# Chunk pairs taken from one batch, fewer and larger loads, and a reordered scan in a fused state-space scan and feed-forward kernel

## The chip, the cores and the metric

The kernel runs on one core of one Trainium2 chip. The metric is the time of one execution in device microseconds. The kernel before takes 173.81 us, the median of three runs between 173.72 and 175.98. The engines are named as in the profile: PE is the matrix engine and PEld its weight loads, DVE the vector engine, ACT the scalar engine, POOL the general-purpose engine, and SP the engine that here only issues transfers. A q behind the name (SPq, ACTq) marks an instruction that issues a DMA.

## The reference

Two layers follow each other. The first is a chunked state-space scan over 4 batches, 8 heads, 768 tokens, with 32 channels of x and 16 of state per head:

```python
for c in range(nc):                       # the reference's chunks have 32 tokens
    cum = np.cumsum(la, axis=-1)          # la = log(clip(a))
    L = np.exp(cum[:, :, :, None] - cum[:, :, None, :]) * causal
    CB = np.einsum('bhin,bhjn->bhij', Cc, Bc)
    y_intra = np.einsum('bhij,bhjd->bhid', CB * L, xc)
    y_inter = np.einsum('bhin,bhnd->bhid', Cc, state) * np.exp(cum)[:, :, :, None]
    y[:, :, sl] = y_intra + y_inter
    Bx = np.einsum('bhjn,bhjd->bhjnd', Bc, xc) * decay_from_j[:, :, :, None, None]
    state = decay_full[:, :, None, None] * state + np.sum(Bx, axis=2)
```

The second takes the 3072 rows of 256 that the scan leaves and is a feed-forward layer with 2048 hidden units:

```python
h = np.maximum(x @ w_in, 0.0)
return (h * h @ w_out).astype(np.float32)
```

## The kernel before, in words

**Units.** A unit of work, a pair, is 256 tokens: one 128-token chunk `c` of two neighbouring batches (`PAIRS`, L106). There are 12 pairs. On the 128 partitions lie 64 token couples of one batch and 64 of the other. The products of decays are made once for all chunks (L318 to L327): `P_sb` is the running product of `a` inside a chunk, `Pinv` its reciprocal, `Ptot` the product of a whole chunk.

**The scan of a pair k** has these phases. `ph_load` (L111) issues the loads of B, C and x on SP, two DMAs per tensor, one for each batch. `ph_prep` (L139) multiplies C by `P_sb` into `cz`, casts B into `Bb`, and multiplies x by `Pinv` into `xs`; from pair 1 on, all three on POOL. `ph_tr` (L162) transposes with six matmuls into PSUM, and DVE copies the result out as `bct` (L171). `ph_mt` (L178) makes the 16 products of C and B, and `ph_mask` (L194) multiplies them by the causal mask on DVE, in four parts, into `mts`. `ph_y` (L202) has 16 matmuls with the old state (L213), 16 that make the state's increment (L224), and 32 that apply `mts` to `xs` (L234). `ph_T` (L244) casts the result on ACT into `T`, and `ph_state` (L251) updates the state on DVE with an addition (L263) and a multiplication (L264).

**One buffer.** `tr`, `mt` and `Y` are all tiles of the tag "A" in the pool `ps_s`, which has one buffer of four PSUM banks. Each of them therefore waits until the one before it has been read to the end.

**The feed-forward of a pair** is eight steps. A step (blk, fp) is `mm1` (L270): four matmuls of 256 columns into `hps` (two buffers), a relu on ACT into `hb` (L278), and a square on DVE into `h2` (L280). `mm2` (L283) is four matmuls (L290) that add a step's part to `ops`. After the eighth step ACT copies `ops` to `osb` (L295) and SP issues four DMAs to the output (L298).

**Order.** It is written out by hand, and every engine works through its own list in that order. The start (L308 to L361 or so) runs pairs 0 and 1 through the scan one behind the other; between their phases ACT issues the loads of the weights, eight DMAs for `w_in` and one for `w_out` in each of five portions (`load_w`, L126), and casts the portions to bf16 (`cast_w`, L302; `w_out` on POOL). Then a loop runs over 96 steps:

```python
mm1(*steps[s])
for fn, args in todo.pop(s, []):
    fn(*args)
if s >= LAG:
    mm2(*steps[s - LAG])
```

`mm2` runs LAG = 3 steps behind `mm1`. The first 16 steps alternate between pairs 0 and 1. The scan of pair k is hung into steps from s0 = 8k - LEAD on, with LEAD = 10: `ph_tr` at s0, `ph_mt` at s0 + 1, the masks at s0 + 2 to s0 + 5, `ph_y` at s0 + 6, `ph_T` and `ph_state` at s0 + 7; `ph_prep` is at s0 - 4 and `ph_load` at s0 - 12.

**Waits of transfers.** The transfers of SP and ACT share eight completion semaphores in turn, so a DMA is issued only when the eighth DMA before it has landed.

## Time and profile before

| What | Value |
|---|---|
| median of the runs | 173.81 us |
| profiled execution, its own time | 173.16 us |
| its span, first to last instruction | 171.4 us |
| PE busy | 111.3 us, 65% |
| PEld busy | 89.5 us, 52% |
| DVE busy | 85.8 us, 50% |
| ACT busy | 72.6 us, 42% |
| POOL busy | 32.0 us, 19% |
| moved by DMA | 14.19 MB in 46,403 packets |
| mean granted clock of PE | 0.995 |

No engine is busy for more than two thirds of the span. The span has a start in which the feed-forward does not run yet, a long middle in which one pair's scan and another's feed-forward go side by side, and a short end. What limits each is read from the waits and the timeline of that stretch, not from the shares of the whole. Busy time of PE counts overlapping matmuls as long as any of them runs, and their ends are modelled.

### The profile page before, as it was taken

How to read it: one execution, taken by the hardware profiler on the slowest of the kernel's cores; microseconds unless marked ns; L12 is line 12 of the kernel's file. 1: busy time of each engine (PE TensorE's matmuls, PEld its weight loads, DVE VectorE, ACT ScalarE, POOL GpSimd, SP SyncE). 2: the span in 40 equal slices, each digit the busy share in tenths (PEclk: the TensorE clock that was granted, in tenths of full speed). 3: DMA queues.
4: the chain of work that ended last, by engine and by line, in shares of the span. 5: the costliest groups of instructions: out<-in, count | busy, mean ns of one | idle time of the engine just before them, and what ended most of it. 6: DMA issues, size and time to landing. Idle time of an engine off the chain costs nothing.

```text
span 171.4 us, 4268 instructions
## 1 busy us (share of the span) xinstructions
PE 111.3 (65%) x1740; PEld 89.5 (52%) x1740; DVE 85.8 (50%) x182; ACT 72.6 (42%) x129; POOL 32.0 (19%) x46
## 2 busy tenths in 40 slices
PE   0132012304976896968958869689685897979970
PEld 0021010203865685756746758568574786768850
DVE  2218007002767474595565745848459455492420
ACT  2001010014855474453535734546346354566740
POOL 4026101502940000314230502204022000000000
PEclk9999999999999999999999999999999999999998
DMA  4775979596000004645624235252351102011012
GB/s 94 144 169 108 198 158 237 106 259 190 2 4 0 4 3 95 136 84 127 115 64 79 53 76 111 46 95 49 78 109 33 33 0 64 3 31 34 18 43 61
DMA packets 46403, 14.19 MB, mean 83 GB/s; under 512 B 39568, under 2 KB 45616, under 8 KB 46384
## 3 DMA queue, kind: packets, MB, share of 16 engines
q1 hardware_dynamic: 42080, 9.54, 29.0%
q10 hardware_dynamic: 4304, 4.39, 8.9%
q8 instruction: 13, 0.21, 0.5%
q14 instruction: 6, 0.05, 0.1%
HBM read 10.77 MB, written 3.15 MB: 81 GB/s over the span
## 4 chain that ended last, share of the span: by engine, by line
PE 32%; DVE 28%; DMA 17%; ACT 10%; issue 5%; SPq 2%; ACTq 2%; DVEq 0%
DVE mts L196 13%; PE ops L290 12%; DVE h L280 11%; PE hps L275 10%; DMA x_nat<-in_x_dram 6%; ACT hb L278 5%; ACT T L247 3%; DMA w_out_f<-in_moe_w_out_dram 3%; DMA w_in_f<-in_moe_w_in_dram 3%; DMA C_nat<-in_C_dram 3%; PE Y L213 2%; PE mt L185 2%; SPq L119 2%; PE Y L234 2%; DMA B_nat<-in_B_dram 2%
## 5 line engine op out<-in xcount | busy, mean ns | idle before, releaser
L278 ACT ACTIVATE hb<-hps 128x512 bf16<-128x512 f32 x96 | 57.5, 602 | 56.6 <-PE hps L275 56.4
L280 DVE TENSOR_TENSOR h<-hb 128x512 bf16<-128x512 bf16 x96 | 45.7, 477 | 47.5 <-ACT hb L278 47.5
L275 PE MATMUL hps<-T,w_in_b 128*128 128x256 bf16 x384 | 59.0, 278 | 9.2 <-ACT T L247 9.2
L290 PE MATMUL ops<-w_out_b,h 128*128 128x256 bf16 x384 | 57.4, 273 | 0.0
L275 PEld LDWEIGHTS <-w_in_b 128*128 128x128 bf16 x384 | 38.1, 99 | 14.9 <-issue 9.7
L290 PEld LDWEIGHTS <-h 128*128 128x128 bf16 x384 | 35.5, 98 | 6.8 <-issue 2.0
L196 DVE TENSOR_TENSOR mts<-mt,cb 128x512 bf16<-128x512 f32 x48 | 32.2, 682 | 2.2 <-PE mt L185 2.2
L144 POOL TENSOR_TENSOR cz<-C_nat,P_sb 128x256 bf16<-128x256 f32 x11 | 7.9, 717 | 57.9 <-DMA C_nat<-in_C_dram 50.7
L166 PE MATMUL tr<-cb,Bb 128*128 128x128 bf16 x24 | 5.0, 230 | 18.8 <-DVE S L260 8.2
L156 POOL TENSOR_TENSOR xs<-x_nat,Pinv 128x512 bf16<-128x512 f32 x12 | 13.7, 1141 | 14.0 <-DMA x_nat<-in_x_dram 12.8
L213 PE MATMUL Y<-bct,S 32*32 32x128 bf16 x160 | 4.0, 216 | 13.7 <-DVE mts L196 13.7
L169 PEld LDWEIGHTS <-cz 128*128 128x128 bf16 x48 | 4.0, 104 | 15.0 <-issue 15.0
L213 PEld LDWEIGHTS <-S 32*32 32x32 bf16 x160 | 3.1, 90 | 15.6 <-issue 15.6
L303 ACT CAST w_in_b<-w_in_f 128x1024 bf16<-128x1024 f32 (+1 forms) x5 | 4.3, 869 | 15.0 <-DMA w_in_f<-in_moe_w_in_dram 15.0
L260 DVE TENSOR_TENSOR S<-Y,Ptot 128x128 bf16<-128x128 f32 x2 | 0.6, 292 | 18.7 <-ACT T L247 18.7
L171 DVE COPY bct<-tr 128x768 bf16<-128x768 bf16 x12 | 6.7, 556 | 5.2 <-PE tr L169 5.2
L247 ACT CAST T<-Y 128x512 bf16<-128x512 f32 x12 | 7.0, 582 | 5.4 <-DMA w_in_f<-in_moe_w_in_dram 5.4
L304 POOL CAST w_out_b<-w_out_f 128x1024 bf16<-128x1024 f32 (+1 forms) x5 | 4.3, 867 | 25.7 <-DMA w_out_f<-in_moe_w_out_dram 16.5
L295 ACT COPY osb<-ops 128x512 f32<-128x512 f32 x12 | 7.0, 583 | 1.2 <-PE ops L290 1.2
L185 PE MATMUL mt<-bct 32*64 32x256 bf16 x192 | 5.7, 303 | 2.2 <-DVE bct L171 2.1
L234 PE MATMUL Y<-mts,xs 64*32 64x128 bf16 x384 | 6.3, 233 | 0.0
L224 PE MATMUL Y<-xs,Bb 64*32 64x64 bf16 x160 | 2.6, 202 | 5.4 <-DVE mts L196 5.4
(28 smaller groups left out, 36.3 us busy)
## 6 DMA issues: line engine op xcount, KB each, us to landing
x_nat<-in_x_dram SPq DMA_DIRECT2D x24, 128.0 KB, 3.2
out_dram<-osb SPq DMA_DIRECT2D x48, 64.0 KB, 2.1
B_nat<-in_B_dram SPq DMA_DIRECT2D x24, 64.0 KB, 2.7
C_nat<-in_C_dram SPq DMA_DIRECT2D x24, 64.0 KB, 2.9
w_in_f<-in_moe_w_in_dram ACTq DMA_DIRECT2D x24, 64.0 KB, 3.2
w_out_f<-in_moe_w_out_dram ACTq DMA_DIRECT2D x3, 512.0 KB, 4.7
w_in_f<-in_moe_w_in_dram ACTq DMA_DIRECT2D x16, 32.0 KB, 2.7
w_out_f<-in_moe_w_out_dram ACTq DMA_DIRECT2D x2, 256.0 KB, 4.2
```

What stands on the lines that cost most here:

```text
L144: e_c.tensor_tensor(out=_fap(czk, 0, [[144, 4], [32, 4], [1, 16]]), in0=_fap(t["C"][:, 0, :], 0, [[16, 4], [64, 4], [1, 16]]), in1=_fap(P_ ...
L156: e_x.tensor_tensor(out=_fap(xs[:, 0, :], 0, [[256, 2], [32, 8], [1, 32]]), in0=_fap(t["x"][:, 0, :], 0, [[32, 2], [64, 8], [1, 32]]), in1 ...
L185: nc.tensor.matmul(mt[64 * u:64 * u + 64, q, r, :, :], bct[32 * q:32 * q + 32, r, 0, u * 64:u * 64 + 64], _fap(bct[32 * q:32 * q + 32, 0, ...
L196: nc.vector.tensor_tensor(out=v["mts"][:, q], in0=v["mt"][:, q], in1=_fap(cb[:, 128:129], 0, [[128, 2], [0, 2], [1, 128]]), op=ALU.mult)
L213: nc.tensor.matmul(Y[32 * q:32 * q + 32, u, g * 128:(g + 1) * 128], S_b[32 * q:32 * q + 32, u, g * 32:(g + 1) * 32], ct_ap(v["bct"], q, g, u),
L234: nc.tensor.matmul(Y[32 * q:32 * q + 32, u, g * 128:(g + 1) * 128], v["xs"][64 * u:64 * u + 64, r, (2 * q + g) * 32:(2 * q + g) * 32 + 32] ...
L247: nc.scalar.copy(out=_fap(t[:, 0, :], 0, [[128, 2], [256, 2], [1, 128]]), in_=Y[:, 0:2, 0:256].rearrange("p u (g i) -> p u g i", g=2))
L275: nc.tensor.matmul(hps[:, j, :], w_in_b[:, g, f * 128:(f + 1) * 128], T[blk][:, g, :], start=(g == 0), stop=(g == 1), skip_group_check=True)
L278: nc.scalar.activation(out=hb, in_=hps, func=AF.Relu)
L280: nc.vector.tensor_tensor(out=h2, in0=hb, in1=hb, op=ALU.mult)
L290: nc.tensor.matmul(ops[blk][:, u, :], h2[:, j, u * 128:(u + 1) * 128], w_out_b[:, f, :], start=(f == 0 and u == 0), stop=(f == 15), skip_g ...
L295: nc.scalar.copy(out=osb, in_=ops.pop(blk))
```

## The change

**Pairs.** A pair is now two neighbouring 128-token chunks of one batch: `PAIRS = [(b, j) for j in range(3) for b in range(4)]`. The 256 tokens are contiguous, so `ph_load` issues one DMA of 128 partitions per tensor instead of two of 64, and the output of a pair is one DMA of 2 KB rows instead of four of 1 KB rows. The second chunk of a pair needs the state that the first leaves, so the state is updated twice inside a pair. As a chain through the state a batch has three pairs instead of six.

**Weights.** `load_w` issues two DMAs per portion instead of nine. The first portion stays on ACT's queue, the other four go to SP's, between the loads of the first pairs. All loads of the start now stand ahead of everything else in the program.

**Scan.** The matmuls of the state's increment leave `ph_y` and become a phase of their own, `ph_u`, right behind the transposes, with the DVE work of the state in it (a sum and a multiplication for each of the two chunks, of 64 columns; no sum where there is no old state). `U` is one more tile of the buffer "A" in the loop. In the start, `tr`, `U` and `Y` of pairs 0 and 1 use the pools of the feed-forward instead of "A". `ph_y` ends with the cast to `T`.

**Feed-forward.** The square of a step leaves `mm1` and is put into the list a step later, behind that step's phases of the scan. LAG goes from 3 to 4, LEAD from 10 to 12, `h2` from 6 to 8 buffers. All eight steps of pair 0 come before those of pair 1. The last two weight portions are cast at steps 2 and 4 (before: three portions, at steps 1, 5 and 9). The masks are at s0 + 2 to s0 + 4.

Where the order of DVE moves: the first rows are DVE's list in the kernel before, for the scan of pair 3 (bct to the last mask) between the squares (h<-hb).

```order
L263 TENSOR_TENSOR z_692<-Y_611,S_271 128x128
L264 TENSOR_TENSOR S_691<-z_692,Ptot 128x128
L280 TENSOR_TENSOR h_7_706<-hb_7_704 128x512
L171 COPY bct_715<-tr_708 128x768
L280 TENSOR_TENSOR h_7_728<-hb_7_726 128x512
L280 TENSOR_TENSOR h_0_759<-hb_0_757 128x512
L196 TENSOR_TENSOR mts_747<-mt_730,cb 128x512
L280 TENSOR_TENSOR h_1_773<-hb_1_771 128x512
L196 TENSOR_TENSOR mts_747<-mt_730,cb 128x512
L280 TENSOR_TENSOR h_2_793<-hb_2_791 128x512
L196 TENSOR_TENSOR mts_747<-mt_730,cb 128x512
L280 TENSOR_TENSOR h_3_827<-hb_3_825 128x512
```

And DVE's list in the changed kernel for the scan of pair 3, where L311 is the square, L206 the mask and L237 to L241 the state.

```order
L185 COPY bct_663<-tr_656 128x768
L311 TENSOR_TENSOR h_3_665<-hb_3_638 128x512
L237 TENSOR_SCALAR S_0_696<-U_679,Ptot 128x64
L240 TENSOR_TENSOR z_1_699<-U_679,S_0_696 128x64
L241 TENSOR_SCALAR S_1_698<-z_1_699,Ptot 128x64
L311 TENSOR_TENSOR h_4_702<-hb_4_654 128x512
L206 TENSOR_TENSOR mts_732<-mt_715,cb 128x512
L311 TENSOR_TENSOR h_5_734<-hb_5_677 128x512
L206 TENSOR_TENSOR mts_732<-mt_715,cb 128x512 x2
L311 TENSOR_TENSOR h_6_749<-hb_6_713 128x512
L206 TENSOR_TENSOR mts_732<-mt_715,cb 128x512
L311 TENSOR_TENSOR h_7_775<-hb_7_745 128x512
```

Before, each mask stands behind the square of its own step; now the square that stands ahead of a mask is of the step before, and the state's update stands between the copy and the masks instead of ahead of the next pair's transposes.

ACT's list at the start of the kernel before (L129 and L132 issue the weights, L303 casts them, L247 writes T, L278 is the first relu):

```order
L325 COPY P_sb<-ptr 128x2x16x6
L129 DMA w_in_f<-in_moe_w_in_dram 32x256 x8
L132 DMA w_out_f<-in_moe_w_out_dram 128x2x256
L152 CAST Bb_160<-B_nat_124 128x256
L129 DMA w_in_f<-in_moe_w_in_dram 32x256 x8
L132 DMA w_out_f<-in_moe_w_out_dram 128x2x256
L303 CAST w_in_b<-w_in_f 128x2x256
L129 DMA w_in_f<-in_moe_w_in_dram 32x512 x8
L132 DMA w_out_f<-in_moe_w_out_dram 128x4x256
L342 COPY Ptot<-pps 128x24
L247 CAST T_269<-Y_220 128x2x2x128
```

ACT's list at the same place of the changed kernel, from the last cast of B on (ahead of these rows stand the copy of P_sb and the other casts of B):

```order
L154 CAST Bb_181<-B_nat_129 128x2x4x16
L369 COPY Ptot<-pps 128x24
L133 CAST w_in_b<-w_in_f 128x2x256
L287 CAST T_289<-Y_0_247 128x4x64
L287 CAST T_289<-Y_1_248 128x4x64
```

The issues have left ACT's list behind P_sb; of the weights only the first portion is still issued by ACT, ahead of that copy.

SP's list in the changed kernel, from the second pair's loads to the third's:

```order
L118 DMA C_nat_127<-in_C_dram 128x8x32
L118 DMA B_nat_129<-in_B_dram 128x8x32
L118 DMA x_nat_131<-in_x_dram 128x8x64
L125 DMA w_in_f<-in_moe_w_in_dram 128x2x256
L128 DMA w_out_f<-in_moe_w_out_dram 128x2x256
L125 DMA w_in_f<-in_moe_w_in_dram 128x2x512
L128 DMA w_out_f<-in_moe_w_out_dram 128x4x256
L118 DMA C_nat_137<-in_C_dram 128x8x32
```

In the kernel before, SP's list holds only a, the pairs' loads (each of these rows twice, with 64 partitions) and the output; now weights stand between the loads of pair 1 and pair 2.

The core of the diff:

```diff
-    LAG = 3
-    LEAD = 10
+    LAG = 4
+    LEAD = 12
...
-    PAIRS = [(c, bp) for c in range(6) for bp in range(2)]
+    PAIRS = [(b, j) for j in range(3) for b in range(4)]
...
-            for u in range(2):
-                b = 2 * bp + u
-                nc.sync.dma_start(
-                    out=dst[64 * u:64 * u + 64],
-                    in_=_dap(src, (b * NH * S + c * L) * w,
-                             [[2 * w, 64], [S * w, NH], [1, 2 * w]]))
+            (eng or nc.sync).dma_start(
+                out=dst, in_=_dap(src, (b * NH * S + j * 256) * w,
+                                  [[2 * w, 128], [S * w, NH], [1, 2 * w]]))
...
-    def load_w(f0, f1):
-        for g in range(2):
-            for q in range(4):
-                nc.scalar.dma_start(
-                    out=w_in_f[32 * q:32 * q + 32, g, f0 * 128:f1 * 128],
-                    in_=moe_w_in[q * 64 + g * 32:q * 64 + g * 32 + 32, f0 * 128:f1 * 128])
-        nc.scalar.dma_start(
+    def load_w(f0, f1, eng):
+        eng.dma_start(
+            out=w_in_f[:, :, f0 * 128:f1 * 128],
+            in_=_dap(moe_w_in, f0 * 128, [[2048, 128], [128 * 2048, 2], [1, (f1 - f0) * 128]]))
+        eng.dma_start(
             out=w_out_f[:, f0:f1, :],
...
+    def ph_u(k):
+        if k < 2:
+            U = [ps_h.tile([128, 64], FP32, tag="hps", name=f"U{k}_{u}", padded_shape=[128, 512])
+                 for u in range(2)]
+        else:
+            t = ps_s.tile([128, 4, 512], FP32, tag="A", name=f"U{k}")
+            U = [t[:, u, 0:64] for u in range(2)]
...
+            if S_u[u] is None:
+                nc.vector.tensor_scalar(out=S_n, in0=U[u], scalar1=ptot, scalar2=None, op0=ALU.mult)
+            else:
+                z = spool.tile([128, 64], FP32, tag="z", name=f"z{k}_{u}")
+                nc.vector.tensor_tensor(out=z, in0=U[u], in1=S_u[u], op=ALU.add)
+                nc.vector.tensor_scalar(out=S_n, in0=z, scalar1=ptot, scalar2=None, op0=ALU.mult)
...
-            for u in range(2):
-                for r in range(2):
-                    nc.sync.dma_start(
-                        out=_dap(out, ((2 * bp + u) * S + c * L + r) * 256, [[512, 64], [1, 256]]),
-                        in_=osb[64 * r:64 * r + 64, u, :])
+            nc.sync.dma_start(out=_dap(out, (b * S + j * 256) * 256, [[512, 128], [1, 512]]), in_=osb)
...
+        ph_load(0)
+        nc.scalar.dma_start(out=cb, in_=cb_d.ap())
+        load_w(0, 2, nc.scalar)
+        ph_load(1)
+        load_w(2, 4, nc.sync)
+        load_w(4, 8, nc.sync)
+        ph_load(2)
+        load_w(8, 12, nc.sync)
+        load_w(12, 16, nc.sync)
+        ph_load(3)
...
-        steps = [(b, f) for f in range(8) for b in range(2)]
-        steps += [(b, f) for b in range(2, NPAIR) for f in range(8)]
+        ph_prep(2)
+        cast_w(4, 8)
+
+        steps = [(b, f) for b in range(NPAIR) for f in range(8)]
...
-        at(1, cast_w, 4, 8)
-        at(5, cast_w, 8, 12)
-        at(9, cast_w, 12, 16)
+        at(2, cast_w, 8, 12)
+        at(4, cast_w, 12, 16)
...
-            at(s0 + 1, ph_mt, k)
+            at(s0 + 1, ph_u, k)
+            at(s0 + 2, ph_mt, k)
             for q in range(4):
-                at(s0 + 2 + q, ph_mask, k, q)
+                at(s0 + 2 + (q + 1) // 2, ph_mask, k, q)
             at(s0 + 6, ph_y, k)
-            at(s0 + 7, ph_T, k)
-            at(s0 + 7, ph_state, k)
         for s in range(len(steps) + LAG):
             if s < len(steps):
                 mm1(*steps[s])
             for fn, args in todo.pop(s, []):
                 fn(*args)
+            if 1 <= s <= len(steps):
+                square(*steps[s - 1])
             if s >= LAG:
                 mm2(*steps[s - LAG])
```

More of the change, by code (lines that the diff above doesn't have):

```diff
@@ new lines @@
+    T = {}
+    def ph_y(k):
+        b, j = PAIRS[k]
+        v = live.pop(k)
+        if k < 2:
+            Y = [ps_h.tile([128, 2, 128], FP32, tag="hps", name=f"Y{k}_{u}", padded_shape=[128, 4, 128])
+                 for u in range(2)]
+        else:
+            t = ps_s.tile([128, 4, 4, 128], FP32, tag="A", name=f"Y{k}")
+            Y = [t[:, u, 0:2, :] for u in range(2)]
+        first = {(u, q): True for u in range(2) for q in range(4)}
+        for u in range(2):
+            S_b = v["S"][u]
+            if S_b is None:
+                continue
+            for g in range(2):
+                for q in range(4):
+                    nc.tensor.matmul(
+                        Y[u][32 * q:32 * q + 32, g, :],
+                        S_b[32 * q:32 * q + 32, g * 32:(g + 1) * 32],
+                        _fap(v["bct"][32 * q:32 * q + 32], 128 + g * 128 + u * 64, [[384, 2], [1, 64]]),
+                        start=first[(u, q)], stop=False, skip_group_check=True,
+                        tile_position=(32 * q, 32 * q))
+                    first[(u, q)] = False
@@ L340 @@
+        nc.scalar.copy(out=Ptot, in_=pps)
         cast_w(0, 2)
[L341 to L344 removed]
+        ph_tr(1)
+        ph_u(0)
         ph_y(0)
[L346 to L351 removed]
         ph_mt(1)
+        ph_u(1)
```

262 lines of the change are left out of this document (120 added, 142 removed).

## The prediction

> **What bounds the kernel now.** I read the page first, then the busy time by stretches, then the timeline of each stretch. The page's engine row and three stretches, with the columns PE, PEld, DVE, ACT and POOL busy, granted clock, DMA share and GB/s:
>
> ```profile
> PE 111.3 (65%) x1740; PEld 89.5 (52%) x1740; DVE 85.8 (50%) x182; ACT 72.6 (42%) x129; POOL 32.0 (19%) x46
> 0.00:40.80 40.80, 6.54 (x148) 4.04 (x149) 9.51 (x20) 4.54 (x9) 10.09 (x18) 1.00 0.73 162
> 101.80:112.80 11.00, 9.00 (x153) 7.35 (x151) 6.74 (x15) 5.56 (x11) 2.06 (x3) 1.00 0.40 78
> 156.30:166.00 9.70, 9.64 (x89) 8.30 (x86) 4.48 (x11) 6.54 (x13) 0.00 (x0) 1.00 0.12 27
> ```
>
> These are three regimes. For 40.8 us PE works 6.5 us. In the middle (one period of eight steps is shown) PE is busy 9.00 of 11.00, and no other engine is fuller. At the end, with no scan left, PE has no gap. So I take the start, the period and the end apart.
>
> The start, from ACT's timeline and PE's (start, duration, engine, and in brackets the idle time before and what ended it):
>
> ```profile
> 5.23 4.38 ACTq L129 DMA_DIRECT2D w_in_f<-in_moe_w_in_dram  x8
> 10.48 4.83 ACTq L129 DMA_DIRECT2D w_in_f<-in_moe_w_in_dram  x8
> 16.02 7.23 ACTq L129 DMA_DIRECT2D w_in_f<-in_moe_w_in_dram  x8
> 24.75 8.85 ACTq L129 DMA_DIRECT2D w_in_f<-in_moe_w_in_dram  x7
> 34.20 5.46 ACTq L129 DMA_DIRECT2D w_in_f<-in_moe_w_in_dram  x8
> 40.17 0.58 ACT L247 CAST T<-Y 128x512 bf16<-128x512 f32 x1 [5.38 <-DMA w_in_f<-in_moe_w_in_dram]
> 40.81 2.72 PE L275 MATMUL hps<-T,w_in_b 128*128 128x256 bf16 x12 [9.22 <-ACT T L247]
> ```
>
> ACT spends some 31 us (4.38 + 4.83 + 7.23 + 8.85 + 5.46) inside issues of `w_in`, and the cast that releases pair 1's feed-forward stands behind them in its list. PE waits 9.22 us for that cast. The start is bound by ACT's list, and behind it by the transfers.
>
> The period, from the timeline around one scan:
>
> ```profile
> 102.77 0.29 DVE L264 TENSOR_TENSOR S<-z,Ptot 128x128 bf16<-128x128 f32 x1
> 102.79 0.22 PE L166 MATMUL tr<-cb,Bb 128*128 128x128 bf16 x1 [0.61 <-DVE z L263]
> 103.12 0.60 PE L290 MATMUL ops<-w_out_b,h 128*128 128x256 bf16 x4
> 103.32 0.56 DVE L171 COPY bct<-tr 128x768 bf16<-128x768 bf16 x1
> 104.08 0.44 PE L185 MATMUL mt<-bct 32*64 32x256 bf16 x16
> 104.45 0.61 PE L290 MATMUL ops<-w_out_b,h 128*128 128x256 bf16 x4
> 110.25 0.41 DVE L280 TENSOR_TENSOR h<-hb 128x512 bf16<-128x512 bf16 x1
> 110.38 0.40 PE L213 MATMUL Y<-bct,S 32*32 32x128 bf16 x16 [1.38 <-DVE mts L196]
> 111.23 0.61 PE L290 MATMUL ops<-w_out_b,h 128*128 128x256 bf16 x4
> ```
>
> From start to start, PE gives 0.33 us to the transposes (102.79 to 103.12), 0.37 to `mt` (104.08 to 104.45) and 0.85 to `Y` with the state's increment (110.38 to 111.23): 1.55 us. It waits 1.38 us for the masks and 0.61 for DVE's state update. The first wait, over the ten pairs in the loop (us in total, times, longest):
>
> ```profile
> PE Y L213 <- DVE mts L196: 13.7, 10, 1.9
> ```
>
> The end gives the pure price of a step:
>
> ```profile
> 157.47 0.60 PE L275 MATMUL hps<-T,w_in_b 128*128 128x256 bf16 x4
> 163.58 0.60 PE L275 MATMUL hps<-T,w_in_b 128*128 128x256 bf16 x4
> 164.02 1.92 PE L290 MATMUL ops<-w_out_b,h 128*128 128x256 bf16 x16
> ```
>
> Seven steps lie between the first two rows: 6.11 / 7 = 0.873 us each, 0.436 for `mm1` or `mm2` alone. A period without waits would be 8 x 0.873 + 1.55 = 8.53 us, against about 11.0 now. So 2.4 us of waiting per pair can be won, and some 20 us in the start.
>
> **The change part by part.**
>
> *The start, by its chain.* ACT issues only the first portion ahead of everything. What then sets step 0 is the scan of pairs 0 and 1, one behind the other. Its rows (transfers with KB and the median us from issue to landing; groups with busy us, mean ns):
>
> ```profile
> 1.63 1.41 SPq L119 DMA_DIRECT2D B_nat<-in_B_dram  x2
> 26.49 0.67 PE L185 MATMUL mt<-bct 32*64 32x256 bf16 x16 [0.65 <-DVE bct L171]
> 27.25 2.48 DVE L196 TENSOR_TENSOR mts<-mt,cb 128x512 bf16<-128x512 f32 x4 [0.81 <-PE mt L185]
> 29.88 0.31 PE L224 MATMUL Y<-xs,Bb 64*32 64x64 bf16 x16 [2.72 <-DVE mts L196]
> 29.96 0.66 PE L234 MATMUL Y<-mts,xs 64*32 64x128 bf16 x32
> x_nat<-in_x_dram SPq DMA_DIRECT2D x24, 128.0 KB, 3.2
> B_nat<-in_B_dram SPq DMA_DIRECT2D x24, 64.0 KB, 2.7
> L278 ACT ACTIVATE hb<-hps 128x512 bf16<-128x512 f32 x96 | 57.5, 602 | 56.6 <-PE hps L275 56.4
> L303 ACT CAST w_in_b<-w_in_f 128x1024 bf16<-128x1024 f32 x3 | 3.1, 1037 | 0.0
> ```
>
> A 128-partition issue has no row; it costs between one old issue and two (1.41 us for two), and I take 1.3, since it names as many pieces as two. C, B and x of pair 0 are then issued by 2.5, 3.8 and 5.1 and land about 2.7, 2.7 and 3.2 later (C has the size of B), at 5.2, 6.5 and 8.3. Casts of B to 7.0; transposes 7.6 (0.33, longer here as `mt` is: 0.67 against 0.37); copy 8.2; `mt` 8.9. DVE's list has the C of pair 1 ahead of the masks: issued by 6.4, landed 9.1, done 9.8 with a multiplication and a small one behind it. Masks to 12.4 (2.48), the next copy 13.0, three state operations of 0.3 to 13.9, `Y` 14.9 (0.31 + 0.66), `T` 15.6. For pair 1 only `U` is left to start then, since it takes the buffers that `T` frees: 16.0, state 16.9, masks 19.5, `Y` 20.5, `T` 21.1. Step 0 thus starts at 21 instead of 40.8. From there ACT's list sets the pace up to step 6: three casts of weights (1.04 each) and five relus (0.6) make 6.1, so step 6 at about 27.3.
>
> *The start, by the transfers.* Step 6 also needs the last portion of `w_in`. The queues' shares in the first 44 us, q1 being SP's and q10 ACT's, and the slowest and the busiest second:
>
> ```profile
> q1 hardware_dynamic: 16064, 2.72, 36.4%
> q10 hardware_dynamic: 4304, 4.39, 34.6%
> 3.00:4.00 1.00, 0.00 (x0) 0.00 (x0) 0.49 (x2) 0.00 (x0) 0.00 (x0) 1.00 0.50 81
> 27.00:28.00 1.00, 0.16 (x8) 0.00 (x0) 0.75 (x2) 0.00 (x0) 0.00 (x0) 1.00 1.24 305
> ```
>
> That is 0.71 x 44 = 31 us of all sixteen engines for the weights (15) and five pairs (16, so 3.2 each). Packets keep their size, so I keep this amount. The loads of pairs 3 and 4 come later, which leaves 25 us ahead of step 6. At a share of 1.24 from 1.2 us on they end at 21.4, at the old mean of 0.71 at 36.4; I take 1.0, nearer to the seconds in which both kinds of load are queued: 26.2, and with the cast's 1.04 us step 6 is at 27.3 again. Bounds for step 6: 25 and 37. I take 27.5.
>
> *The middle.* From step 6 on PE has 90 `mm1` and 94 `mm2`: 184 x 0.436 = 80.3 us. Ten scans cost 1.55 each, less the transposes of pair 2, which are done by then: 15.2. `U` standing alone adds a fill between two matmul groups; by the 0.85 us it shares now it costs from 0 to 0.31, and I take 0.1 per pair: 1.0. Sum 96.5.
>
> What is waited for then: the squares' own waits in DVE's list go, since the square ahead of a mask has its relu a step behind it. Masks stand at s0 + 2 to s0 + 4 and `Y` at s0 + 6, so PE has eight half steps, 3.5 us, between `mt` and `Y`; DVE needs four masks (0.62 each) and two squares (0.41): 3.3. That hides the masks by 0.2 us, and the 0.3 us of old-state matmuls that open `Y` don't need them. `U` waits for the copy of `tr` (0.56 and the hand-over) behind 0.87 us of `mm2` and `mm1`: hidden. `mt` waits until DVE has read `U`: a square, then three operations of up to 0.29, about 1.1 us against 0.87. So I leave 0.2 us per pair there and 0.2 at `Y`: 4.0 in all. The bounds are 0 and today's 24.
>
> LAG 4 hides a square's later place: it has two steps before its `mm2`. The queue positions of POOL do not change what is late: the preparation of a pair is 16 steps ahead of its `mm1`.
>
> *The end.* PE stops at 164.02 + 1.92 = 165.94, and the span ends 5.45 us later, behind the copy to `osb` and four output issues. Such four, in the period:
>
> ```profile
> 108.38 2.43 SPq L298 DMA_DIRECT2D out_dram<-osb  x4
> ```
>
> One issue instead of four saves three of 2.43 / 4 = 0.6 us: 3.6 us are left.
>
> *Sum.* 27.5 + 96.5 + 4.0 + 3.6 = 131.6 us of span. The profiled execution took 173.16 at a span of 171.4, so 1.8 lie around it: 133.4; and the median of the runs was 0.65 above that execution: 134. I forecast 134.
>
> **The rivals.**
>
> *DVE becomes late at `Y`.* POOL's preparation slows a square beside it:
>
> ```profile
> 107.44 1.08 POOL L156 TENSOR_TENSOR xs<-x_nat,Pinv 128x512 bf16<-128x512 f32 x1 [1.13 <-PE hps L275]
> 108.04 0.75 DVE L280 TENSOR_TENSOR h<-hb 128x512 bf16<-128x512 bf16 x1
> ```
>
> The square took 0.75 us beside POOL's 1.08, 0.41 alone. The masks are hidden by only 0.2 us, and two squares stand between them: 2 x 0.34 late at every `Y`, and as much at `mt`, where a square stands ahead of the state, would be 1.0 to 1.4 per pair, so 144 to 148. Against it: POOL works 2.06 of 11.00 us, and may fall elsewhere. [...] The row above shows 0.34 of a possible 1.08.
>
> *The transfers stay as slow as they are.* If one queue reaches only the old mean share of 0.71, step 6 is at 37 and the time 143.5. For it: nothing in the packets changes, and in the second shown with only SP's small packets the share is 0.50. In this case the merging does not do what it says. Against: the busy seconds above 1.
>
> *The hand-overs through the one buffer.* The other sign: `tr`, `U`, `mt`, `Y` are now four tenants of "A" instead of three, and each must wait for DVE or ACT to read the one before. If PE overlapped nothing, a pair would pay the copy 0.56, four state operations 1.16, masks and the squares among them 3.3, and `T` 0.58: 5.6 us per pair, so 134 - 4 + 56 = 186, slower. It decides from (173.8 - 130) / 10 = 4.4 us per pair on. Against it speaks that half steps of 0.436 us stand between all of them, and that today's two hand-overs cost 2.0.
>
> **How the numbers follow.** The forecast's own case, 128 to 139, gets 0.62: within it step 6 moves by a few us and the waits per pair between 0 and 0.8. DVE late gets 0.18 (140 to 148, and rarely to 154), slow transfers 0.10 (139 to 144), the hand-overs 0.03, and 0.05 is for a start better than its chain or for less work at the end: 25 + 96.5 + 0 + 3.6 + 2.4 = 127.5 is the floor. 0.02 is left for a gain that is eaten up. The range from 128 to 149 leaves out about 0.15. A change of this kernel can be told from no change from about 2% on; faster by more gets 0.95, the same 0.02, slower 0.03.
>
> **What would show it.** In the changed kernel's timeline: step 0's `hps` near 21 us and step 6's near 27; ACT without long issues; DMA share near 1 up to 26 us. In the middle, stretches of eight steps of about 8.9 us with PE busy nearly all of it; the wait of `Y` for `mts` far below 1.38 a time, and that of `tr` for `z` gone, with at most a small one at `mt` in its place. In the end 3.6 us after PE's last matmul. It is wrong if `Y` or `mt` waits above 0.8 us per pair, if squares beside POOL grow in number, if step 6 starts after 31, or if the granted clock leaves 1.00 as PE's gaps close.

## The result and the profile after

The changed kernel takes 131.8 us, the median of runs between 130.9 and 132.3, against 173.76 us for the kernel before on the same chip. The ratio is 0.760, with a 95% interval from 0.753 to 0.767. The forecast was 134 us, the range 128 to 149. The profiled execution took 131.33 us at a span of 129.5 us, 41.9 us less than before. The times told here and below are medians of all runs; the ratios leave out runs in a slower state that some executions show (in one set below 155.67 and 172.75 us, at mean granted clocks of 0.79 and 0.70).

The page of the changed kernel, its engine row:

```profile
PE 111.8 (86%) x1740; PEld 87.8 (68%) x1740; DVE 90.4 (70%) x201; ACT 75.7 (58%) x134; POOL 31.6 (24%) x54
```

PE does as much as before (111.8 us against 111.3), but in 129.5 us instead of 171.4. The three regimes of the prediction, and between the second and the third one period of the middle, by stretches (the columns as in the prediction: PE, PEld, DVE, ACT, POOL busy, granted clock, DMA share, GB/s):

```profile
0.00:27.25 27.25, 13.18 (x214) 7.94 (x215) 14.06 (x33) 10.87 (x22) 9.04 (x17) 1.00 0.94 230
27.25:125.90 98.65, 98.58 (x1526) 79.90 (x1526) 76.38 (x169) 64.26 (x113) 22.52 (x37) 1.00 0.34 78
60.65:69.55 8.90, 8.90 (x152) 7.12 (x150) 7.50 (x17) 5.74 (x11) 2.50 (x4) 1.00 0.42 91
125.90:129.50 3.60, 0.00 (x0) 0.00 (x0) 0.00 (x0) 0.56 (x1) 0.00 (x0) 0.89 0.19 73
```

From 27.25 us on PE has no gap at all: 98.58 of 98.65 us. A period of eight steps takes 8.90 us instead of 11.0. To split the gain I need the same step in the kernel before; its PE timeline has step 0, the first of pair 0, and step 6 in these rows:

```profile
30.55 1.04 PE L275 MATMUL hps<-T,w_in_b 128*128 128x256 bf16 x4
45.68 0.60 PE L275 MATMUL hps<-T,w_in_b 128*128 128x256 bf16 x4
```

- Start: step 6 moved from 45.68 to 27.25, 18.4 us. (Step 0 stood at 30.55; the 40.8 us that the prediction gives for it are step 1, the first of pair 1.)
- Middle: from step 6 to the end of PE's last matmul it was 165.94 - 45.68 = 120.3 us; now 125.84 - 27.25 = 98.6. That is 21.7 us.
- End: 5.45 us behind PE's last matmul became 3.6, which is 1.8 us less.

The start, from the timelines of ACT and PE in the changed kernel:

```profile
19.68 0.65 ACT L287 CAST T<-Y 128x256 bf16<-128x256 f32 x2 [3.82 <-PE Y L276]
26.15 1.04 ACT L133 CAST w_in_b<-w_in_f 128x1024 bf16<-128x1024 f32 x1 [0.45 <-DMA w_in_f<-in_moe_w_in_dram]
20.11 3.24 PE L301 MATMUL hps<-T,w_in_b 128*128 128x256 bf16 x16 [0.42 <-ACT T L287]
24.46 0.61 PE L301 MATMUL hps<-T,w_in_b 128*128 128x256 bf16 x4 [1.11 <-ACT w_in_b L133]
27.25 0.61 PE L301 MATMUL hps<-T,w_in_b 128*128 128x256 bf16 x4 [0.25 <-ACT w_in_b L133]
```

Pair 1's cast to `T` now waits only for PE's `Y`. Step 0 starts at 20.11, step 6 at 27.25, behind the cast of the last `w_in` portion. That cast waited 0.45 us for its transfer: the two limits of the start, ACT's list and the transfers, end within half a microsecond of each other.

One scan of the middle, from the timelines of PE and DVE in the changed kernel (L185 copies `bct`, L206 is a mask, L311 a square):

```profile
60.65 0.22 PE L181 MATMUL tr<-cb,Bb 128*128 128x128 bf16 x1
60.98 0.60 PE L321 MATMUL ops<-w_out_b,h 128*128 128x256 bf16 x4
61.42 0.60 PE L301 MATMUL hps<-T,w_in_b 128*128 128x256 bf16 x4
61.95 0.25 PE L224 MATMUL U<-xs,Bb 64*32 64x64 bf16 x16
66.14 0.69 DVE L206 TENSOR_TENSOR mts<-mt,cb 128x512 bf16<-128x512 f32 x1
66.74 2.29 DVE L311 TENSOR_TENSOR h<-hb 128x512 bf16<-128x512 bf16 x4
67.11 0.40 PE L264 MATMUL Y<-bct,S 32*32 32x128 bf16 x16
67.79 0.61 PE L321 MATMUL ops<-w_out_b,h 128*128 128x256 bf16 x4
```

None of PE's rows has an idle time in brackets. The last mask ends at 66.83. `Y` takes the buffer of `mt`, so even its first matmuls can begin only when this mask has read `mt` to the end. They begin at 67.11, 0.28 us behind it; where the mask is what `Y` waits for, as in two of the experiments below, the distance is 0.05 us. So the masks are hidden by some 0.2 us. The waits that answer to those shown of before, over the whole execution:

```profile
PE Y L276 <- DVE mts L206: 1.8, 4, 0.8
```

These four times are those of pair 1 in the start, one for each mask; the loop has none (13.7 us in ten before). There is no row for `tr` behind the state, and none for `mt` or `U` in the loop.

### The profile page after: what moved, and what is told of

Read it like the earlier page. It is cut to its first block, busy times and chain, and to the rows that moved or that the text cites. A ratio compares the mean times of both kernels' runs of the same rounds, so it can differ in the third digit from the quotient of the medians.

```text
span 129.5 us, 4148 instructions
## 1 busy us (share of the span) xinstructions
PE 111.8 (86%) x1740; PEld 87.8 (68%) x1740; DVE 90.4 (70%) x201; ACT 75.7 (58%) x134; POOL 31.6 (24%) x54
## 4 chain that ended last, share of the span: by engine, by line
PE 76%; SPq 11%; DMA 8%; ACT 1%; issue 1%
PE ops L321 34%; PE hps L301 30%; SPq L118 8%; DMA w_in_f<-in_moe_w_in_dram 6%; PE mt L195 3%; PE Y L276 3%; PE Y L264 2%; DMA cf<-const_f 2%; SPq L125 2%; PE tr L183 2%; PE U L224 1%; SPq L128 1%; ACT w_in_b L133 1%; PE tr L181 1%; ACT osb L326 0%
## 5 line engine op out<-in xcount | busy, mean ns | idle before, releaser
L311 DVE TENSOR_TENSOR h<-hb 128x512 bf16<-128x512 bf16 x96 | 45.9, 500 | 9.4 <-ACT hb L305 9.4
L321 PEld LDWEIGHTS <-h 128*128 128x128 bf16 x384 | 34.7, 98 | 7.0 <-issue 2.0
L206 DVE TENSOR_TENSOR mts<-mt,cb 128x512 bf16<-128x512 f32 x48 | 31.5, 685 | 2.8 <-PE mt L195 2.7
L142 POOL TENSOR_TENSOR cz<-C_nat,P_sb 128x256 bf16<-128x256 f32 x10 | 6.8, 682 | 40.4 <-DMA C_nat<-in_C_dram 28.8
L185 DVE COPY bct<-tr 128x768 bf16<-128x768 bf16 x12 | 6.7, 556 | 13.4 <-PE tr L183 13.4
L290 ACT CAST T<-Y 128x512 bf16<-128x512 f32 x10 | 5.9, 586 | 1.3
L156 POOL CAST Bb<-B_nat 128x128 bf16<-128x128 f32 x20 | 5.8, 319 | 1.8 <-DMA B_nat<-in_B_dram 1.7
L264 PE MATMUL Y<-bct,S 32*32 32x128 bf16 x160 | 4.6, 225 | 1.9 <-DVE S L237 1.9
L276 PEld LDWEIGHTS <-xs 64*32 64x32 bf16 x384 | 3.4, 95 | 3.8 <-issue 1.7
L183 PE MATMUL tr<-cb,cz 128*128 128x128 bf16 x48 | 5.9, 235 | 0.0
L264 PEld LDWEIGHTS <-S 32*32 32x32 bf16 x160 | 2.3, 91 | 4.3 <-DVE S L237 2.2
L287 ACT CAST T<-Y 128x256 bf16<-128x256 f32 x4 | 1.3, 376 | 6.5 <-PE Y L276 6.5
## 6 DMA issues: line engine op xcount, KB each, us to landing
C_nat<-in_C_dram SPq DMA_DIRECT2D x12, 128.0 KB, 3.5
B_nat<-in_B_dram SPq DMA_DIRECT2D x12, 128.0 KB, 4.1
```

The costliest lines, as they stand in the source:

```text
L183: nc.tensor.transpose(tr[:, r, 1 + g, :], v["cz"][:, r, 112 * g:112 * g + 128], eye_b)
L206: nc.vector.tensor_tensor(out=v["mts"][:, q], in0=v["mt"][:, q], in1=_fap(cb, 128, [[128, 2], [0, 2], [1, 128]]), op=ALU.mult)
L264: nc.tensor.matmul(Y[u][32 * q:32 * q + 32, g, :], S_b[32 * q:32 * q + 32, g * 32:(g + 1) * 32], _fap(v["bct"][32 * q:32 * q + 32], 128 + ...
L276: nc.tensor.matmul(Y[u][32 * q:32 * q + 32, g, :], v["xs"][64 * u:64 * u + 64, r, h * 32:h * 32 + 32], v["mts"][64 * u:64 * u + 64, q, r, ...
L311: nc.vector.tensor_tensor(out=h2, in0=hb, in1=hb, op=ALU.mult)
L321: nc.tensor.matmul(ops[blk][:, r, :], h2[:, i, r * 128:(r + 1) * 128], w_out_b[:, f, :], start=(f == 0 and r == 0), stop=(f == 15), skip_g ...
```

## The experiments

Ratios are to the kernel before, run beside each on the same chip, with 95% intervals. The changed kernel's own is 0.760 [0.753, 0.767]; in another run of it, told below, 0.762 [0.756, 0.768].

**The square in its own step again.** The changed kernel with

```diff
+                square(*steps[s])
...
-            if 1 <= s <= len(steps):
-                square(*steps[s - 1])
```

behind `mm1`.

> The changed kernel with one thing undone: each square stands in DVE's list at its own step again, ahead of that step's scan work; LAG stays 4, the masks, the state update and all loads stay as changed. If the later place of the squares is what removed the waits of the middle, the copy of the transposes stands behind a square whose relu ends about 1.2 us after the step's mm1, so U waits about 0.6 us, and mt, behind the state, about 0.9: 1.5 us for each of ten pairs, 147 us (143 to 150), with DVE idle on relus. If the new places of masks and state are enough by themselves, 131 to 134 us.

Measured: 147.87 us, ratio 0.847 [0.837, 0.857]. This one line is worth 16.1 us by the medians, 0.087 x 174 = 15 us by the ratios. Its waits:

```profile
DVE h L311 <- ACT hb L305: 43.6, 64, 1.9
PE Y L264 <- DVE mts L206: 7.5, 10, 0.9
PE U L224 <- DVE bct L185: 4.6, 9, 0.5
```

DVE stands 43.6 us for relus again (47.5 in the kernel before, 9.4 in the changed one), and what stands behind a square in its list, the copy of the transposes and the masks, comes late. The amount came out as expected, the place only in part: PE pays it at `U` and at `Y`, and hardly at `mt` (1.3 us once), where the larger part was expected.

**The later square alone, in the kernel before** (with LAG 4 and eight buffers for `h2`, as the changed kernel has):

```diff
-    LAG = 3
+    LAG = 4
...
+            if 1 <= s <= len(steps):
+                square(*steps[s - 1])
```

> The kernel before with one part of the change alone: squares one step later in DVE's list, LAG 4 and eight h2 buffers. If the squares' waits for their relus were what made the masks late, Y's wait of 1.38 us per pair falls to about 0.3 and the wait of the transposes for the state update stays near 0.6: ten pairs win 10 to 14 us, 160 to 164 us. If the masks' schedule or the state's place was the cause, it stays within 2% of the kernel before, 170 to 176 us.

Measured: 160.94 us, ratio 0.923 [0.915, 0.932], so 0.077 x 174 = 13 us alone. Its waits:

```profile
PE Y L213 <- DVE mts L196: 0.6, 1, 0.6
PE tr L166 <- DVE z L263: 4.9, 8, 0.6
```

The masks' 13.7 us are gone. The wait of `tr` for the state, 4.9 us in eight times, stands as it did in the kernel before: a later square does not touch it.

**The state's increment next to `Y` again.** The changed kernel with

```diff
-            at(s0 + 1, ph_u, k)
-            at(s0 + 2, ph_mt, k)
+            at(s0 + 1, ph_mt, k)
...
+            at(s0 + 5, ph_u, k)
```

and the masks half a place earlier with `mt`.

> The changed kernel with the state's increment and update (U, sum, multiplication) moved in the loop from one step behind the transposes to one step ahead of Y; mt and the masks move one step forward into the gap. If the place beside the transposes matters, U now waits in the one buffer for the last mask, and Y for the chain of four state operations of about 0.26 us against 0.87 us of matmuls: 0.2 to 0.6 us per pair, 134 to 138 us. If only the squares' place and the spread of the masks matter, the time stays at 131 to 133 us.

Measured: 134.8 us, ratio 0.772 [0.762, 0.781].

```profile
PE Y L264 <- DVE z L240: 2.5, 3, 0.9
```

PE waits 2.5 us in three scans for the state's operations. The median is 2 to 3 us above the changed kernel's, about these waits; the intervals overlap, so that only the waits are told for certain.

**The masks one step apart**, at s0 + 2 to s0 + 5, instead of within three steps:

```diff
-                at(s0 + 2 + (q + 1) // 2, ph_mask, k, q)
+                at(s0 + 2 + q, ph_mask, k, q)
```

> The changed kernel with the masks one per step at s0 + 2 to s0 + 5 again, squares still a step later. Now three squares stand among the masks and the last one ends about when the masks' part of Y begins: at most 0.2 us per pair, 131 to 134 us. If the closer masks are what removed the wait of Y, 0.8 us or more per pair come back: 140 us or more.

Measured: 133.19 us, ratio 0.771 [0.766, 0.775].

```profile
PE Y L264 <- DVE mts L206: 1.4, 3, 0.7
```

The slack of 0.2 us is used up: the last mask starts 5.83 us behind the transposes instead of 5.49, and in all ten scans `Y` follows its end by 0.05 us. In only three of them is the wait long enough to be listed. The medians differ by 1.4 us, and the intervals touch. Once the square is a step later, the masks' place is worth little.

**Only the queue of the weights, in the kernel before.** Their 45 issues go to SP, with the pairs' loads between, all ahead of the rest; nothing is merged.

```diff
-                nc.scalar.dma_start(
+                eng.dma_start(
...
+        load_w(0, 2, nc.sync)
+        ph_load(1)
+        load_w(2, 4, nc.sync)
```

> The kernel before with one part of the change alone, and that without its merging: all loads of the start stand ahead of everything, and the weights are issued on SP between the pairs' loads, in the old nine DMAs per portion; ACT issues only the two constants. If ACT's list was what held the start, T of pair 1 comes some 14 us earlier (near 25 us instead of 40), and the time is 156 to 163 us, the rest of the old 173 being held by SP's 77 issues. If the transfers themselves set the start, or if merging is what matters, the time stays above 169 us.

Measured: 162.88 us, ratio 0.939 [0.931, 0.946]. From ACT's timeline:

```profile
21.59 0.59 ACT L247 CAST T<-Y 128x512 bf16<-128x512 f32 x1 [1.38 <-PE Y L234]
33.48 1.04 ACT L303 CAST w_in_b<-w_in_f 128x1024 bf16<-128x1024 f32 x1 [4.65 <-DMA w_in_f<-in_moe_w_in_dram]
```

With ACT's list free, the cast that released the feed-forward stands at 21.59 instead of 40.17, and step 6 at 28.48 instead of 45.68. But ACT waits for portions that land late (4.65 us in this row, 5.45 and 4.73 us ahead of the first two casts), and the scan behind it too: `mt` waits 4.34 us at 36.01. The move alone gives some 11 us of the start's 18; the rest needs loads that land earlier.

**The other half: `w_in` in 32-partition pieces**, eight DMAs instead of one, in the changed kernel, on the same queues.

```diff
-        eng.dma_start(
-            out=w_in_f[:, :, f0 * 128:f1 * 128],
...
+        for g in range(2):
+            for q in range(4):
+                eng.dma_start(
+                    out=w_in_f[32 * q:32 * q + 32, g, f0 * 128:f1 * 128],
```

> The changed kernel with each portion of w_in issued as eight DMAs of 32 partitions again, on the queues where the change has put them, so that only the merging is undone: 35 more issues. If the start is bound by the amount that the transfers move (DMA share 0.94 up to step 6), the issues hide behind it and the time is 132 to 135 us. If the number of issues sets the start, 28 more issues of about 0.43 us on SP put the last portion some 10 us later: 139 to 143 us.

Measured: 137.58 us, ratio 0.792 [0.784, 0.799], between the two. The first 32 us by stretches:

```profile
0.00:32.00 32.00, 14.76 (x213) 8.72 (x214) 13.45 (x31) 9.89 (x21) 9.44 (x17) 0.95 0.79 180
```

And from the timelines of SP, ACT and PE an issue, the last cast of `w_in` and step 6:

```profile
7.60 5.15 SPq L127 DMA_DIRECT2D w_in_f<-in_moe_w_in_dram  x8
31.89 1.04 ACT L135 CAST w_in_b<-w_in_f 128x1024 bf16<-128x1024 f32 x1 [2.19 <-DMA w_in_f<-in_moe_w_in_dram]
32.99 0.61 PE L303 MATMUL hps<-T,w_in_b 128*128 128x256 bf16 x4 [0.55 <-ACT w_in_b L135]
```

The amount moved by then is nearly the same (0.79 x 32 = 25.3 us of all engines, against 0.94 x 27.25 = 25.6), but it takes until about 32: eight issues held SP for up to 5.15 us, and the DMA engines are less full meanwhile. The number of issues counts, where I had expected it to hide. The eight issues that stay on ACT also push the copy of `P_sb` from 5.20 to 9.02 and step 0 to 21.65; but the last cast waits 2.19 us for its transfer, so this does not set step 6.

**The pairs' loads in halves**, two DMAs of 64 partitions for each tensor, in the changed kernel.

```diff
-            (eng or nc.sync).dma_start(
+            for u in range(2):
+                (eng or nc.sync).dma_start(
+                    out=dst[64 * u:64 * u + 64], ...
```

> The changed kernel with each pair's B, C and x loaded as two DMAs of 64 partitions again. If the start is bound by what the transfers move, SP's 24 issues instead of 12 for the first four pairs (0.6 us each, against 0.4 to 0.9 for a whole one) cost at most what is left of its slack: 132 to 134 us, and the middle stays without waits, since loads run 17 steps ahead. If the one DMA per tensor carries part of the win by itself, 135 us or more.

Measured: 135.81 us, ratio 0.787 [0.781, 0.793]: the rival's side. From SP's timeline and PE's:

```profile
2.61 1.37 SPq L119 DMA_DIRECT2D B_nat<-in_B_dram  x2
27.08 0.68 PE L302 MATMUL hps<-T,w_in_b 128*128 128x256 bf16 x4 [2.84 <-ACT w_in_b L134]
31.01 0.60 PE L302 MATMUL hps<-T,w_in_b 128*128 128x256 bf16 x4
```

Step 4 waits 2.84 us for a cast whose portion lands late, and step 6 starts at 31.01. The middle has no waits of its own. So the merged loads matter through the start, since SP's added issues put the last portions back (the last one of `w_in` is issued at 22.15 instead of 18.81). Part of it is PE's rate, which comes up below: behind this wait it is at half (granted clock 0.57 from 27 to 31 us), and from step 4 to step 6 it takes 3.93 us, against 2.54 in the changed kernel without its wait of 0.25.

**More of `w_in` ahead of pair 2's loads** (4 to 12; 12 to 16 follows right behind those loads, ahead of the later `w_out`), the casts of 4 to 12 ahead of pair 1's `T`, and LAG 5:

```diff
-        load_w(4, 8, nc.sync)
+        load_wi(4, 8, nc.sync)
+        load_wi(8, 12, nc.sync)
```

> A variant that aims below the changed kernel: the w_in portions 8 to 12 and 12 to 16 are loaded ahead of the w_out portions, which are needed four steps later, the casts of w_in 4 to 12 stand ahead of T of pair 1 where ACT idles 3.8 us, and LAG is 5. If the last portion of w_in and ACT's three casts hold steps 2 to 6, step 6 starts near 25 to 26 us instead of 27.25 and the time falls by 1 to 2 us, 130 to 131 us. If the transfers of pair 2 or of w_out take their place as the last wait, it stays at 131.5 to 133 us.

Measured: 131.67 us, ratio 0.759 [0.755, 0.764]: no gain. From PE's timeline:

```profile
25.87 0.61 PE L313 MATMUL hps<-T,w_in_b 128*128 128x256 bf16 x4
30.97 0.29 PE L276 MATMUL Y<-bct,S 32*32 32x128 bf16 x8 [0.53 <-DVE mts L218]
123.25 2.78 PE L333 MATMUL ops<-w_out_b,h 128*128 128x256 bf16 x24
```

Step 6 starts 1.4 us earlier, as meant. Of that 0.53 goes at the first `Y` of the loop, which now waits for masks, and 0.44 at the end, where LAG 5 leaves six `mm2` behind the last `mm1` instead of five. The remaining 0.5 is spread over four later scans, 0.1 to 0.2 us longer each; no wait is listed there, and the cause stays open.

**Alternating first steps.** The start's last limit is that steps 4 to 6 want the last portions. With pairs 0 and 1 alternating, as before the change, the portions are wanted half as fast:

```diff
-        steps = [(b, f) for b in range(NPAIR) for f in range(8)]
+        steps = [(b, f) for f in range(8) for b in range(2)]
+        steps += [(b, f) for b in range(2, NPAIR) for f in range(8)]
...
-        at(2, cast_w, 8, 12)
-        at(4, cast_w, 12, 16)
+        at(5, cast_w, 8, 12)
+        at(9, cast_w, 12, 16)
```

> The first sixteen steps alternate between pairs 0 and 1 again, as in the kernel before, and the last two weight portions are cast at steps 5 and 9; all else as in the changed kernel. Theory: in the changed kernel steps 0 to 6 take 7.1 us (20.11 to 27.25) because they wait for the last w_in portions, whose data the DMA engines deliver until about 26. With the steps alternating, step 6 needs only the second portion of four blocks; the pace is then ACT's: one cast of 1.06 and five relus of 0.6 behind 20.2, so step 6 at about 24.4, 2.9 us earlier, and the last portions are needed from step 12, at about 29, when they are there. Time 128.5 to 130 beside 131 to 132. Rival: what is late next takes it back: pair 3's loads, the last of SP's list at the start, land after 28, its preparation on POOL and its transposes at step 12 wait for them, and the middle starts no earlier: 131 to 132.

> The changed kernel once more, unaltered, on the same chip, so that the alternation has a neighbour to be compared with: 131 to 132.5.

Measured: 131.14 us, ratio 0.752 [0.747, 0.757], against 133.06 us and 0.762 [0.756, 0.768] for the unaltered changed kernel beside it. A second time the alternating kernel had 130.53 us and 0.750 [0.745, 0.756] (below). It is the fastest version tried, by about 1%; the intervals touch, and the gain is smaller than the 2 to 3 us expected. Why, and why two executions of the changed kernel differ by 1.5 us of span (129.5 and 131.0), PE's timeline shows. First the repeated changed kernel:

```profile
20.00 3.58 PE L301 MATMUL hps<-T,w_in_b 128*128 128x256 bf16 x16 [0.42 <-ACT T L287]
24.35 1.04 PE L301 MATMUL hps<-T,w_in_b 128*128 128x256 bf16 x4 [0.77 <-ACT w_in_b L133]
28.58 0.60 PE L301 MATMUL hps<-T,w_in_b 128*128 128x256 bf16 x4
```

And the alternating one:

```profile
19.85 4.44 PE L301 MATMUL hps<-T,w_in_b 128*128 128x256 bf16 x20 [0.43 <-ACT T L287]
24.09 0.31 PE L181 MATMUL tr<-cb,Bb 128*128 128x128 bf16 x1
26.45 0.60 PE L301 MATMUL hps<-T,w_in_b 128*128 128x256 bf16 x4
36.37 0.44 PE L195 MATMUL mt<-bct 32*64 32x256 bf16 x16 [0.45 <-DVE z L240]
```

After the start's sparse matmuls PE runs at half its rate. Sixteen or twenty matmuls take about 0.89 us per four (3.58 / 4, 4.44 / 5; 0.436 later), a transpose 0.31 (0.22 later). The change to the full rate fell ahead of 24.46 in the first profiled execution (its step 4 took 0.61) and near 28 in the second (step 4 took 1.04 at 24.35), and step 6 started at 27.25 and 28.58. With alternating steps no portion is waited for, but the first five steps run at half rate, so step 6 comes at 26.45 instead of the 24.4 expected.

Against the first execution of the changed kernel that is still 0.8 us gained, and the next scan takes it back, as the rival said, though by another way. From the transposes of pair 3 to those of pair 4 it takes 9.55 us (33.27 to 42.82; 8.75 in the changed kernel), and PE ends at 125.82 instead of 125.84. Of this, 0.45 us is the wait at `mt` above, for the state. DVE's list has the reason:

```profile
34.56 1.30 DVE L311 TENSOR_TENSOR h<-hb 128x512 bf16<-128x512 bf16 x1
```

A square that takes 0.42 us elsewhere stands ahead of the state and takes 1.30 beside a multiplication of POOL from 34.52 to 35.58.

**PE kept busy through the start.** The alternating kernel with 17 matmuls of 256 columns more, whose result nobody reads, beside the alternating kernel once more:

```diff
+            nc.tensor.matmul(filler[0][:, 0:256], eye_b, cb[:, 0:256], start=True, stop=True)
...
+        fill(6)
         ph_y(0)
...
+        fill(6)
         ph_y(1)
+        fill(2)
```

> The kernel with alternating first steps, and 17 matmuls of 256 columns more on PE whose result nobody reads: six where PE waits for the state of pair 0, six before Y of pair 1, one behind each of its first three masks, two ahead of step 0. Theory: PE runs at half its rate after the sparse matmuls of the start. In the kernels so far the first four or five steps come 0.87 us apart, transposes take 0.31 and masked products 0.67 until about 24 to 28 us, and 0.44, 0.22 and 0.44 from then on, and the moment of the change differs by 3 us between two executions of one kernel. If PE is kept busy from 11.6 us on, the change falls ahead of step 0: the transposes of pair 2 take 0.22, step 0 to 4 take about 3.1 us instead of 4.4 (one relu of 0.6 each on ACT), step 6 starts at 25 instead of 26.5, and the time is 129 to 130.3 beside 130.7 to 131.4. Rival: the rate follows something else than PE's own work (the time since the start, the transfers), so the steps stay 0.87 us apart, and the added matmuls only delay Y: 131 to 132.

> The kernel with alternating first steps once more, unaltered, on the same chip, as the neighbour of the one with added matmuls: 130.7 to 131.5; over several executions the moment at which PE's rate doubles may differ.

Measured: 130.87 us with the added matmuls, ratio 0.752 [0.747, 0.757], and 130.53 us without, 0.750 [0.745, 0.756]: no difference. What the added matmuls did to the rate is seen in PE's timeline:

```profile
11.76 1.46 PE L254 MATMUL filler<-cb 128*128 128x256 bf16 x6
15.26 0.83 PE L254 MATMUL filler<-cb 128*128 128x256 bf16 x6
25.15 0.60 PE L311 MATMUL hps<-T,w_in_b 128*128 128x256 bf16 x4
```

And in two single microseconds by stretches, where the last column but two is the granted clock:

```profile
16.00:17.00 1.00, 0.38 (x10) 0.19 (x9) 0.97 (x3) 0.00 (x0) 0.00 (x0) 1.00 1.05 150
18.00:19.00 1.00, 0.87 (x27) 0.46 (x30) 1.00 (x3) 0.00 (x0) 0.44 (x1) 0.52 1.21 317
```

Six of them take 1.46 us at 11.76 and 0.83 at 15.26: after some 3 us of nearly unbroken work PE was at the full rate. So the rate follows PE's own work: `mt` right behind the first six takes 0.57 us at 14.28, and 0.67 at 14.34 in the kernel without them. But between the masks of pair 1 PE is busy for only 0.38 and 0.80 of the two microseconds from 16 to 18, and from 18 on the granted clock is 0.5 again, for some 3 us. That the thin stretch brings the fall is likely by this order and was not tested apart. Step 6 starts at 25.15, as expected, in a span of 128.3 us; but the executions of the kernel without added matmuls reach from 128.0 to 129.6 us of span, so this one execution shows no gain. Here, too, the scan of pair 3 is long (9.44 us), with a wait of 0.6 us for masks. A denser filling was not tried.

## Why the prediction was right

*The start* (forecast: step 0 at 21, step 6 at 27.5; measured 20.11 and 27.25). The cause was named rightly: the cast to `T` behind 31 us of issues in ACT's list. Moving the issues alone brings that cast from 40.17 to 21.59. The transfers came out as worked out, too: 25.6 us of all engines by step 6 (25 forecast), at a share of 0.94 (1.0 taken). Three terms inside were off and nearly cancel, so that a difference of 0.25 us is in part luck.

- The issues on SP, taken as 1.3 us for 128 partitions: the first four (0.73 to 2.28 us) took 0.39 to 0.91 us, later ones in the start up to 3.61 us, as SP's timeline of the changed kernel shows.

```profile
1.65 0.59 SPq L118 DMA_DIRECT2D B_nat<-in_B_dram  x1
24.22 3.61 SPq L118 DMA_DIRECT2D x_nat<-in_x_dram  x1
```

- The landing, taken as 2.7 us for B. It took twice as long: B of pair 0 is issued by 2.24, and its cast, which waits for it, starts at 7.80, where the chain had it landed at 6.5.

```profile
7.80 0.50 ACT L154 CAST Bb<-B_nat 128x128 bf16<-128x128 f32 x2 [2.28 <-DMA B_nat<-in_B_dram]
```

  The scan made up for it further on. `Y` of pair 0 starts at 13.71, behind the first of the three state operations and not behind all, and `U` of pair 1 at 15.19, before `T` of pair 0 is through (16.0 in the chain). So step 0 came 0.9 us earlier than forecast.

- Steps 0 to 6 were put at 6.1 us, all ACT's. They took 7.1, since PE gave the first four 3.24 us (3.58 in the repeated run) and then waited 1.11 and 0.25 for casts. The same half rate stands in the prediction's own row of the kernel before, 2.72 us for twelve matmuls at 40.81, and I read it only as a wait's end.

The rival of slow transfers (a share of 0.71, step 6 at 37) is refuted by the share. How near it lay is seen in the two kernels with smaller loads: 0.79 in the first 32 us with `w_in` in pieces, and step 6 at 31.01 with halved pair loads. Fewer DMAs are part of the gain, 4 to 5 us for the pairs and 5 to 6 for `w_in` by medians and ratios, each undone alone. With halved pair loads some 1.4 us of that are PE's rate, which fell back to half behind the wait for a late portion. With pieces it fell too (mean granted clock 0.95 in the first 32 us), but there the last cast waits for its transfer in any case.

*The middle* (forecast 96.5 of work + 4.0 of waits = 100.5; measured 98.6). The mechanism was right: with the square a step later PE's wait for masks ends. Undone, it costs 15 to 16 us; done alone in the kernel before, it gives 13 us. The two terms were off in opposite ways. The waits of 0.2 at `mt` and 0.2 at `Y` per pair were 0, with little to spare: `mt` starts 0.06 us behind the addition that reads `U` for the last time (63.14; 62.86 + 0.22), and the slack at `Y` is the 0.2 us of the forecast. That the old-state matmuls ahead of it don't need the masks was wrong: they need `mt`'s buffer, as the waits at L264 in the experiments show. And the pure period of 8.53 with 0.1 for the fill of `U` was 8.90. Of that, 16 x 0.436 = 6.98 are `mm1` and `mm2`; transposes take 0.33 (60.65 to 60.98) and `Y` 0.68 (67.11 to 67.79). The rest is `U` and `mt`, and about 0.1 us at each switch from the feed-forward to a phase of the scan, where the profile records no wait: `mm1` at 61.42 would end at 61.86 by its 0.436, and `U` begins at 61.95.

The rival of a late DVE did not come about at PE. But POOL holds squares as it assumed, and longer than the prediction read. One such pair of rows in the changed kernel, and the squares' group on its page:

```profile
85.56 1.06 POOL L162 TENSOR_TENSOR xs<-x_nat,Pinv 128x512 bf16<-128x512 f32 x1 [1.95 <-DMA x_nat<-in_x_dram]
85.61 1.29 DVE L311 TENSOR_TENSOR h<-hb 128x512 bf16<-128x512 bf16 x1
L311 DVE TENSOR_TENSOR h<-hb 128x512 bf16<-128x512 bf16 x96 | 45.9, 500 | 9.4 <-ACT hb L305 9.4
```

POOL's multiplication ends at 86.62, and the square 0.28 us later, at 86.90. All 15 squares of this execution that took more than 0.45 us end 0.27 to 0.28 us behind an instruction of POOL, and so do the 15 of the kernel before. The prediction's own row is one of them (POOL ends at 108.52, the square at 108.79): its 0.34 us were not lost out of 1.08, but out of the 0.48 that POOL still had to run when the square began. So each of these squares lasted until POOL's instruction was through. At a mean of 500 ns, against 0.42 us alone, the 96 squares lose some 8 us in all. No run shows the 20 us that the 154 us among the chances put on top of the forecast; in their place stand these 8 us, on DVE. PE does not pay them, because nearly all of the long multiplications fall beside squares that stand behind the last mask (66.74 in the scan shown), where nothing waits for them. The prediction had only "may fall elsewhere" for this, so the place was luck. In pair 3 of the alternating kernel it falls ahead of the state, and PE waits.

The rival of the hand-overs (186 us) is refuted by the same rows: four tenants of one buffer, and PE waits for none. The place of the state's increment contributes little: 2.5 us of waits where it stands next to `Y`.

*The end* (forecast 3.6 us, measured 3.6): PE's last row ends at 125.84, and the span at 129.5.

```profile
123.49 2.35 PE L321 MATMUL ops<-w_out_b,h 128*128 128x256 bf16 x20
```

*The sum* was 2.1 us too long in the span (131.6 against 129.5): 0.25 in the start, 1.9 in the middle. None of what the prediction named as signs against it appeared: the squares slowed by POOL are 15 as before, though longer. Five expectations of experiments missed: that the number of issues hides (twice), that an earlier step 6 is passed on to the end, and the gains of the alternation and of the added matmuls.

## What to carry to other kernels

Where two engines work through ordered lists, look at what stands ahead of an instruction in its list, not at its engine's busy share: the square ahead of each mask cost 13 to 16 us on an engine that was half idle. When a start is bound by one list, count at once what the second limit is; here the transfers lay within half a microsecond behind, and moving the issues without merging them gave 11 of 18 us. What merging alone gives, with the weights left on ACT, was not run. And a price measured in full flow (here 0.436 us for four matmuls) need not hold where the engine has just been idle (0.89 in the start): read it from rows of that stretch.

## What the runs showed of the hardware

- After the sparse matmuls of the start PE ran at half its rate (0.89 us for four matmuls of 256 columns, 0.436 later), and the moment of the change differed between executions of one kernel (before 24.46 and near 28 us here), worth 1.3 us at step 6 (27.25 and 28.58). The granted clock in the profile shows 1.00 in those stretches all the same, up to the first rise (1.00 from 20 to 24 us in both executions). Where the rate fell again later, it does show it: 0.50 with the added matmuls, and 0.50 to 0.57 in the kernels with smaller loads, behind the wait for a portion. With the added matmuls PE worked nearly unbroken from 11.8 us on, and by 15.3 it was at the full rate (1.46 us for six at 11.76, 0.83 for six at 15.26).
- The issue of pair 0's B as 128 partitions took 0.59 us, its two halves of 64 together 1.37; for x it was 0.91 against 1.67. But a later issue of 128 partitions held SP for 3.61 us (x at 24.22 in the changed kernel); why it took so long was not shown.
- A switch of PE from 128-row matmuls to the small tiles of the scan cost about 0.1 us that no wait records (0.09 ahead of `U` and of `Y` in the scan shown, reckoned from 0.436 us for `mm1`).
